# Stage Y on the two halves of TensorE: pairs of 48-row matmuls of 47 columns in place of single 112-row matmuls of 94

## The chip, the core and the metric

The kernel runs on one core of a Trainium2 chip. The metric is the device time of one execution in microseconds (us); lower is better. Executions of one kernel agree within about 0.4% of their median (one set of eleven runs of the kernel before: 794.43 to 799.02 around 796.20); a run far above the others, at a lower granted clock, is called slow and is left out.

## The reference

Eight batches of 3008 tokens with 256 features go through a filter in frequency space along the tokens, then each token through a two-layer network with a squared ReLU.

```python
X = np.fft.rfft(x, axis=1)                     # x: (8, 3008, 256)
Y = X * (filt_r + 1j * filt_i)[None]
y = np.fft.irfft(Y, n=3008, axis=1)
h = np.maximum(y.reshape(-1, 256) @ w_in, 0.0)   # w_in: (256, 2048)
out = (h * h) @ w_out                            # w_out: (2048, 256)
```

## The kernel before

The Fourier transforms are matrix products: 3008 = 64 x 47, and the inverse ends in stage Y, a transform of length 47 for each of the 64 values of n1. Its input, per n1, is 48 rows (24 frequencies, real and imaginary) of 256 features. Everything is in float16 with float32 sums.

Stage Y takes two n1 at a time, an even and an odd one. Their rows lie one above the other in a tile of 112 partitions (48, then 16 of zeros, then 48), and a table of 112 x 94 with zeros in half of its places keeps the two apart: 47 columns belong to the even n1 and 47 to the odd one, interleaved.

```python
def read_z(b, c, ks=(0, 1)):
    zt = ztiles[c]                                    # [112, 8, 256]
    v = dZ[b].rearrange("(q j) d -> q j d", j=NM)
    for k in ks:
        nc.sync.dma_start(out=zt[64 * k:64 * k + 48],
                          in_=v[48 * k:48 * k + 48, 8 * c:8 * c + 8, :])

def unit_y(b, n):                                     # n = 0..15 in each batch
    g, dt = divmod(n, 2)
    ...
    ps = psF(f"psY_{b}_{n}")                          # one PSUM bank (in the prologue, every other from psO)
    ...
    for jj in range(4):
        nc.tensor.matmul(ps[:, 94 * jj:94 * jj + 94],
                         zt[:, 4 * (g % 2) + jj, dt * 128:(dt + 1) * 128],
                         sSY, start=True, stop=True)
    ...
    if dt == 0 or (b == 0 and g > 5):
        nc.scalar.copy(out=o, in_=pv)                 # 376 columns
    else:
        nc.vector.tensor_copy(out=o, in_=pv)
```

A batch has 16 units of four matmuls. There are two psF banks, and stages A, B and P use the same two. The units are wedged between the pieces of the two network layers. One token group of 512 tokens has eight slots; a slot is four matmuls of the first layer, then what is planned for its place 0, then eight matmuls of the second layer (of the group before), then what is planned for its place 1:

```python
for s in range((NG + 1) * SLOTS):
    ffn_g1(g, k)          # 4 matmuls of 512 columns, into psH; then a relu on ScalarE
    run(work, s, 0)
    ffn_g2(g - 1, k)      # 8 matmuls of 256 columns, into psO
    run(work, s, 1)
    ffn_out(g - 1, k)
    ffn_sq(g, k)          # the square, on VectorE
```

So nearly every unit of stage Y has full-array matmuls on both sides.

## Time and profile before

| kernel before | |
|---|---|
| time, median of 3 runs | 795.54 us (795.02 to 796.49) |
| TensorE busy | 98% of the span |
| VectorE, ScalarE busy | 69%, 70% |
| stage Y: matmuls, weight loads | 512, 512 |
| one unit of four on the chain | 0.17 us |
| copies out of PSUM | 128 of 376 columns |

The busy times of engines other than TensorE cost nothing here, and the busy time of stage Y's matmuls (42.3 us) counts time that they share with their neighbours. What to read is the chain, which gives to each piece only the time by which it pushed the end. The lines are in the prediction.

### The profile page before, as it was taken

To read this page: it belongs to the slowest core of one execution; us is meant where nothing else is said; L and a number is where in the kernel's file an instruction comes from. 1 tells how busy PE (TensorE), PEld (TensorE's weight loads), DVE (VectorE), ACT (ScalarE), POOL (GpSimd) and SP (SyncE) were. 2 spreads that over 40 slices of the span, in tenths; PEclk is the share of its full clock that TensorE was granted. 3 is DMA by queue.
4 is the path that set the end of the run, shared out by engine and by line. 5 is a ranking of instruction groups with operands and counts; after the bars stand their busy time and mean duration, and the time that the engine had idled before them with its cause. 6 is when DMAs were issued, how large, how long until landed. Compare 5 with 4: busy or idle time off the path is not lost.

```text
span 795.8 us, 14801 instructions
## 1 busy us (share of the span) xinstructions
PE 783.1 (98%) x6102; PEld 553.7 (70%) x6102; DVE 552.2 (69%) x898; ACT 554.9 (70%) x708; POOL 24.4 (3%) x27
## 2 busy tenths in 40 slices
PE   8989999999999999999999999999999999999998
PEld 5846677667676676867778676776777667776666
DVE  6946995579855897559965699557985589554342
ACT  3856776767777677767777677676776767766664
POOL 3710000000000000000000000000000000000000
PEclk9989999999999999999999999999999999999999
DMA  9994555336724467055471555525563342511111
GB/s 352 361 277 134 130 151 139 92 126 165 202 58 107 158 165 181 30 164 151 124 183 49 171 153 137 129 71 156 156 170 97 87 142 80 123 48 41 40 41 54
DMA packets 88139, 107.32 MB, mean 135 GB/s; under 512 B 6288, under 2 KB 78864, under 8 KB 83856
## 3 DMA queue, kind: packets, MB, share of 16 engines
q1 hardware_dynamic: 87864, 106.19, 46.9%
q8 instruction: 48, 0.79, 0.4%
q10 hardware_dynamic: 144, 0.18, 0.1%
q14 instruction: 19, 0.16, 0.1%
q0 software_dynamic: 64, 0.00, 0.0%
HBM read 58.12 MB, written 48.23 MB: 134 GB/s over the span
## 4 chain that ended last, share of the span: by engine, by line
PE 93%; DMA 3%; ACT 1%; DVE 1%; issue 0%; POOL 0%; SPq 0%; ACTq 0%; DVEq 0%; POOLq 0%
PE psO L577 40%; PE psH L560 39%; PE psA L359 3%; PE psY L530 3%; PE psB L443 2%; PE psP L494 2%; PE warm L274 1%; DMA ut<-dU 1%; DMA xw<-in_x_dram 1%; PE psf L293 1%; DMA dZ<-ze 1%; ACT h L564 1%; PE psf L296 0%; DMA dU<-u 0%; PE psA L380 0%; ACT sF L303 0%
## 5 line engine op out<-in xcount | busy, mean ns | idle before, releaser
L564 ACT ACTIVATE h<-psH 128x1024 f16<-128x1024 f32 x376 | 385.2, 1025 | 189.7 <-PE psH L560 188.2
L577 PE MATMUL psO<-sWout,h 128*128 128x256 f16 x3008 | 388.6, 272 | 0.0
L560 PE MATMUL psH<-yt,sWin 128*128 128x512 f16 (+7 forms) x1728 | 386.9, 351 | 1.7 <-DVE yt L539 0.8
L577 PEld LDWEIGHTS <-h 128*128 128x128 f16 x3008 | 290.6, 98 | 77.3
L568 DVE TENSOR_TENSOR h<-h 128x1024 f16<-128x1024 f16 x376 | 253.7, 685 | 100.8 <-ACT h L564 99.2
L560 PEld LDWEIGHTS <-sWin 128*128 128x128 f16 x1728 | 159.5, 98 | 101.7 <-issue 3.5
L451 DVE TENSOR_TENSOR prod<-psB,sF 128x1024 f16<-128x1024 f32 x84 | 102.4, 1219 | 5.9 <-PE psB L443 5.6
L539 DVE CAST yt<-psY 128x376 f16<-128x376 f32 x62 | 33.9, 549 | 57.4 <-PE psY L530 57.4
L365 DVE CAST u<-psA 96x512 f16<-96x512 f32 x50 | 34.3, 687 | 47.3 <-PE psA L359 45.1
L496 ACT CAST ze<-psP 128x512 f16<-128x512 f32 x84 | 49.2, 586 | 17.8 <-PE psP L494 15.9
L588 ACT COPY ost<-psO 128x512 f32<-128x512 f32 (+1 forms) x96 | 55.7, 580 | 6.7 <-PE psO L577 5.3
L530 PEld LDWEIGHTS <-zt 112*128 112x128 f16 x512 | 34.9, 98 | 12.1 <-issue 2.0
L530 PE MATMUL psY<-sC,zt 112*128 112x94 f16 x512 | 42.3, 205 | 0.6 <-DMA zt<-dZ 0.3
L465 DVE TENSOR_TENSOR yf<-prod,yf 128x512 f16<-128x512 f16 x84 | 35.7, 425 | 2.9
L443 PE MATMUL psB<-ut,sSB 128*128 128x256 f16 x192 | 36.5, 272 | 0.6 <-DMA ut<-dU 0.5
L359 PE MATMUL psA<-x,sC 94*96 94x512 f16 x96 | 36.6, 382 | 0.0
L443 PEld LDWEIGHTS <-sSB 128*128 128x128 f16 x192 | 18.6, 98 | 20.9 <-issue 1.7
L494 PE MATMUL psP<-yf,sSP 128*128 128x256 f16 x168 | 32.1, 273 | 0.2 <-ACT yt L537 0.2
L537 ACT CAST yt<-psY 128x376 f16<-128x376 f32 x66 | 30.7, 468 | 1.1 <-PE psY L530 0.6
L338 DVE CAST x<-x 94x2048 f16<-94x2048 f32 x24 | 29.2, 1216 | 0.0
L363 ACT CAST u<-psA 96x512 f16<-96x512 f32 x50 | 28.6, 572 | 0.0
L458 DVE COPY yf<-prod 64x512 f16<-64x512 f16 x84 | 24.3, 289 | 2.9
(63 smaller groups left out, 255.9 us busy)
## 6 DMA issues: line engine op xcount, KB each, us to landing
x<-in_x_dram SPq DMA_DIRECT2D x20, 768.0 KB
zt<-dZ SPq DMA_DIRECT2D x64, 192.0 KB
dU<-u SPq DMA_DIRECT2D x28, 384.0 KB
dZ<-ze SPq DMA_DIRECT2D x28, 384.0 KB
out_dram<-ost SPq DMA_DIRECT2D x66, 128.0 KB
out_dram<-ost SPq DMA_DIRECT2D x31, 256.0 KB
ut<-dU SPq DMA_DIRECT2D x7, 1024.0 KB
xw<-in_x_dram SPq DMA_DIRECT2D x4, 1024.0 KB
```

The source lines that it names most:

```text
L359: nc.tensor.matmul(ps[0:96, :], sSA, x16s[(b, c)][:, m, :], start=True, stop=True)
L443: nc.tensor.matmul(ps[:, i * D:(i + 1) * D], sSB[:, 2 * p + i, :], uts[b][:, 2 * p + i, :], start=True, stop=True)
L451: nc.vector.tensor_mul(out=prod, in0=ps.rearrange("p (a d) -> p a d", d=D).unsqueeze(1).to_broadcast([128, 2, 2, D]), in1=sF[:, :, 2 * p:2 ...
L465: nc.vector.tensor_add(out=yf, in0=prod[:, 0], in1=yf)
L494: nc.tensor.matmul(ps[:, i * D:(i + 1) * D], sSP[:, 2 * p + i, :], yf[:, i, :], start=True, stop=True)
L496: nc.scalar.copy(out=zes[(b, c)][:, 2 * i6:2 * i6 + 2, :], in_=ps.rearrange("p (a d) -> p a d", d=D))
L530: nc.tensor.matmul(ps[:, 94 * jj:94 * jj + 94], zt[:, 4 * (g % 2) + jj, dt * 128:(dt + 1) * 128], sSY, start=True, stop=True)
L560: nc.tensor.matmul(ps[:, i, o:o + n], sWin[:, dt, jt * 128:(jt + 1) * 128], yts[b][:, dt, r:r + n], start=(dt == 0), stop=(dt == 1))
L564: nc.scalar.activation(out=h2[:, 2 * s:2 * s + 2, :], in_=ps, func=AF.Relu)
L568: nc.vector.tensor_mul(out=v, in0=v, in1=v)
L577: nc.tensor.matmul(pso[g][:, t % 2, :], h2s[g][:, jt, t * 128:(t + 1) * 128], sWout[:, jt, :], start=(jt == 0), stop=(jt == NJT - 1))
L588: nc.scalar.copy(out=ost[:, h0:h0 + step, :], in_=pso[g][:, h0:h0 + step, :])
```

## The change

The intent is to stop multiplying with zeros. The even n1 keeps partitions 0 to 63, the odd one 64 to 127, and each gets a matmul of 48 rows and 47 columns of its own. By the Trainium skill ("TensorEngine Tiling (Array Packing)", Overview and Gotcha 1) TensorE can work as two halves where 64 rows or fewer are summed, and the halves must write to different banks. So an even and an odd matmul may run at the same time: 47 columns of streaming in place of 94. A unit takes both psF banks, one for each half, and to fill them it takes eight n1 pairs rather than four. A batch has eight units in place of 16.

```diff
-    SY = np.zeros((32, 2, 2, N2, 2))
+    SP = SP.transpose(0, 1, 2, 4, 3, 5)              # order of rows of the stage before
+    SY = np.zeros((NC, 2, N2))
 ...
-    C0[:, 1376:1470] = SY.reshape(128, 94)
+    for i in range(2):
+        C0[64 * i:64 * i + 48, 1376:1376 + N2] = SY.reshape(48, N2)
 ...
-    for t in ztiles:
-        nc.vector.memset(t[32:64], 0.0)
 ...
-        for jj in range(4):
-            nc.tensor.matmul(ps[:, 94 * jj:94 * jj + 94],
-                             zt[:, 4 * (g % 2) + jj, dt * 128:(dt + 1) * 128],
-                             sSY, start=True, stop=True)
+        for j in range(8):
+            for i in range(2):
+                p = slice(64 * i, 64 * i + 48)
+                nc.tensor.matmul(ps[i][:, N2 * j:N2 * j + N2],
+                                 zts[(b, c)][p, j, dt * 128:(dt + 1) * 128],
+                                 sSY[p], start=True, stop=True)
 ...
+        engs = (nc.scalar.copy, nc.vector.tensor_copy)
+        for i in range(2):
+            (engs[0] if b == 0 and c == 3 else engs[i])(
+                out=o[:, 2 * c + i], in_=ps[i][:, 0:376].rearrange("p (j a) -> p a j", j=8))
 ...
-            for n in range(4, 16):
-                put(n if n < 8 else n + 2 if n < 12 else 2 * n - 7, n % 2, unit_y, 0, n)
+            for n in range(2, 8):
+                put((4, 6, 10, 12, 17, 20)[n - 2], 1, unit_y, 0, n)
 ...
-                put(44 + n // 2, n % 2, unit_y, b, n)
+                put(44 + n, 0, unit_y, b, n)
```

(Cut: the reads of Z with the new row order, the choice of banks in the prologue, and the plan of batch 1.)

More of the change, by code (lines that the diff above doesn't have):

```diff
@@ L84, in _build_consts @@
                 SP[1, f, c, i, 1] = sg * cs
-    SY = np.zeros((32, 2, 2, N2, 2))
+    SP = SP.transpose(0, 1, 2, 4, 3, 5)
+    SY = np.zeros((NC, 2, N2))
     for c in range(NC):
         th = 2 * np.pi * c * n2 / N2
-        for i in range(2):
-            SY[c + c // 12 * 4, i, 0, :, i] = np.cos(th)
-            SY[c + c // 12 * 4, i, 1, :, i] = -np.sin(th)
+        SY[c, 0] = np.cos(th)
+        SY[c, 1] = -np.sin(th)
     PF = np.zeros((128, 6, 2, 2, 32))
@@ L205 @@
     sSA = sC0[0:94, 1280:1376]
-    sSY = sC0[0:112, 1376:1470]
+    sSY = sC0[:, 1376:1376 + N2]
     ident = sC0[:, 576:704]
@@ L504, with read_z @@
     ztiles = [const.tile([112, 8, D], F16, name=f"zt_{c}") for c in range(4)]
-    for t in ztiles:
-        nc.vector.memset(t[32:64], 0.0)
-    def read_z(b, c, ks=(0, 1)):
+    def read_z(b, c):
         zt = ztiles[c]
-        v = dZ[b].rearrange("(q j) d -> q j d", j=NM)
-        for k in ks:
-            nc.sync.dma_start(out=zt[64 * k:64 * k + 48],
-                              in_=v[48 * k:48 * k + 48, 8 * c:8 * c + 8, :])
+        v = dZ[b].rearrange("(q i j) d -> i q j d", i=2, j=NM)
+        for i in range(2):
+            nc.sync.dma_start(out=zt[64 * i:64 * i + 48], in_=v[i, :, 8 * c:8 * c + 8, :])
@@ L514, in read_z @@
         zts[(b, c)] = zt
     def unit_y(b, n):
-        g, dt = divmod(n, 2)
+        c, dt = divmod(n, 2)
         if n == 0:
             yts[b] = p_y.tile([128, 2, S], F16, tag="yt", name=f"yt_{b}")
-        zt = zts[(b, g // 2)]
-        if not prologue[0]:
-            ps = psF(f"psY_{b}_{n}")
+        if prologue[0] and dt:
+            ps = [psO(f"psY_{b}_{n}_{i}").rearrange("p a d -> p (a d)") for i in range(2)]
         else:
-            ps = psF(f"psY_{b}_{n}") if dt == 0 else psO(f"psY_{b}_{n}").rearrange("p a d -> p (a d)")
+            ps = [psF(f"psY_{b}_{n}_{i}") for i in range(2)]
@@ L526, in unit_y @@
         if prologue[0]:
-            for k in range(2):
-                nc.tensor.matmul(ps[:, 128 * k:128 * k + 128], zero, zero, start=True, stop=True)
-        for jj in range(4):
-            nc.tensor.matmul(ps[:, 94 * jj:94 * jj + 94],
-                             zt[:, 4 * (g % 2) + jj, dt * 128:(dt + 1) * 128],
-                             sSY, start=True, stop=True)
-        r, t = g // 2 * 2, g % 2 * 4
-        o = yts[b].rearrange("p d (r a t) -> p d r a t", r=8, t=8)[:, dt, r:r + 2, :, t:t + 4]
@@ L535, in unit_y @@
-        pv = ps[:, 0:376].rearrange("p (j a i) -> p i a j", j=4, i=2)
-        if dt == 0 or (b == 0 and g > 5):
-            nc.scalar.copy(out=o, in_=pv)
-        else:
-            nc.vector.tensor_copy(out=o, in_=pv)
+            for k in range(4):
+                nc.tensor.matmul(ps[k % 2][:, 0:128], zero, zero, start=True, stop=True)
+        for j in range(8):
[4 more added lines that the diff above has]
+                                 sSY[p], start=True, stop=True)
@@ L542 @@
+        o = yts[b].rearrange("p d (r a t) -> p d r a t", r=8, t=8)[:, dt]
+        engs = (nc.scalar.copy, nc.vector.tensor_copy)
+        for i in range(2):
+            (engs[0] if b == 0 and c == 3 else engs[i])(
+                out=o[:, 2 * c + i], in_=ps[i][:, 0:376].rearrange("p (j a) -> p a j", j=8))
     h2s, pso = {}, {}
@@ L640, in fft_plan @@
                     put(r, 1, load_x, b + 1, c + 2)
-        for n in range(16):
+        for n in range(8):
             if b == 1:
-                put(38 + n // 2 if n > 3 else 39, n % 2, unit_y, b, n)
+                put((39, 39, 40, 41, 42, 43, 44, 45)[n], n % 2, unit_y, b, n)
             else:
-                put(44 + n // 2, n % 2, unit_y, b, n)
+                put(44 + n, 0, unit_y, b, n)
         return plan
@@ L718 @@
         write_u(1, c)
-    for n in range(4):
+    for n in range(2):
         unit_y(0, n)
```

## The prediction

> **What bounds the kernel now.** I read the page first: busy shares, then the chain that ended last, then the costliest groups.
>
> ```profile
> PE 783.1 (98%) x6102; PEld 553.7 (70%) x6102; DVE 552.2 (69%) x898; ACT 554.9 (70%) x708; POOL 24.4 (3%) x27
> ...
> PE 93%; DMA 3%; ACT 1%; DVE 1%; issue 0%; POOL 0%; SPq 0%; ACTq 0%; DVEq 0%; POOLq 0%
> ...
> L539 DVE CAST yt<-psY 128x376 f16<-128x376 f32 x62 | 33.9, 549 | 57.4 <-PE psY L530 57.4
> ...
> L530 PEld LDWEIGHTS <-zt 112*128 112x128 f16 x512 | 34.9, 98 | 12.1 <-issue 2.0
> L530 PE MATMUL psY<-sC,zt 112*128 112x94 f16 x512 | 42.3, 205 | 0.6 <-DMA zt<-dZ 0.3
> ...
> L537 ACT CAST yt<-psY 128x376 f16<-128x376 f32 x66 | 30.7, 468 | 1.1 <-PE psY L530 0.6
> ```
>
> TensorE is busy 98% of the span and is 93% of the chain; VectorE and ScalarE stand at 70%. So time of TensorE is time of the kernel, and stage Y (line 530) is 512 matmuls on 112 rows with 94 columns, each behind its own weight load. Its 42.3 us busy are not its cost: a single matmul is shown as 205 ns, but they overlap each other and their neighbours. What one costs on the path is read from the chain, in a stretch of the steady part:
>
> ```profile
> by line: PE psO L577 43.8%; PE psH L560 43.7%; PE psY L530 13.3%
> ...
> 223.29 0.17 PE psY L530 x4
> 223.46 0.88 PE psO L577 x8
> 224.34 0.17 PE psY L530 x4
> 224.51 0.88 PE psH L560 x8
> ...
> 232.86 0.87 PE psH L560 x8
> 233.74 0.87 PE psO L577 x8
> ```
>
> The columns are start, length, what. The chain is TensorE alone, without a hole. Four matmuls of stage Y take 0.17 us, some 42 ns each; eight of 256 columns take 0.88, so 110 ns each. The difference, 68 ns over 162 columns, is 0.42 ns a column; 94 columns are then 39 ns and 3 ns are left as a fixed part. So stage Y streams already: its weight loads, shown as 98 ns each, are wholly hidden. Its cost on the path is 512 x 42 = 21.4 us, 2.7% of 795.5. That is the whole prize if the stage cost nothing.
>
> How fast can a load and a matmul follow each other? Between 127 and 140 us a batch border falls inside a token group, and half of the eight matmuls of a piece have 64 columns only:
>
> ```profile
> L560 PE MATMUL psH<-yt,sWin 128*128 128x448 f16 x24 | 6.0, 352 | 0.0
> L560 PE MATMUL psH<-yt,sWin 128*128 128x64 f16 x24 | 2.8, 192 | 0.3 <-DVE yt L539 0.3
> ...
> 130.69 0.88 PE psH L560 x8
> ```
>
> Such a piece has 4 x 448 + 4 x 64 = 2048 columns, as many as eight of 256, and takes the same 0.88 us. So a pair of load and matmul goes through in about 64 x 0.42 + 3 = 30 ns with nothing added: a load of 128 columns repeats in 30 ns or less. How much less the trace can't say.
>
> **What the Trainium skill says.** "TensorE: Matmul & The Clock Gate", Back-to-back issue gap, gives N / 2.4 + 2.5 ns for a warm matmul; 94 columns make 41.7, and the trace has 42. It agrees. The same page, LDWEIGHTS, gives P / 1.2, thus 107 ns for 128 columns; the 98 ns of the records are near it, but loads repeat within 30 ns here, so as a rate it does not hold in this trace. The same page, Part 3 (Packing small matmuls), says that matmuls on different row groups run concurrently, with starts some 4 ns apart, and that a load overlaps a running matmul when the row groups differ. No run here shows that yet: nothing in this kernel has 64 rows or fewer. "TensorEngine Tiling (Array Packing)", Key Properties, says that changing the tiling mode drains TensorE, without a figure; its Gotcha 1 says that row tiles must write different banks, which is why the change takes two.
>
> **The change part by part.**
>
> TensorE, removed: 512 loads and 512 matmuls of 94 columns on 112 rows, half of whose products are with zeros: 21.4 us. Added: 1024 loads of 128 columns on 48 rows and 1024 matmuls of 47 columns, alternating between rows 0 to 63 and 64 to 127. One alone would take 47 x 0.42 + 3 = 23 ns. If both of a pair run at once and loads stay hidden, 512 pairs x 23 = 11.8 us: a gain of 9.6. That is the floor of the time, 786. I don't expect all of it: a pair now needs two loads and two matmuls issued in 23 ns, while the densest that the trace shows is one of each in 30. If loads of the two halves overlap so that a pair takes those 30 ns, it is 15.4 us and the gain is 6. This is my main case.
>
> Switching in and out of the half mode: 64 units, each between full-array matmuls, so some 128 changes. If a change lets the pipeline run dry, it exposes part of the 205 - 39 = 166 ns by which a matmul's record is longer than its streaming. Each 10 ns per change is 1.3 us. I put in 15 ns as a weighted mean of "nothing" and "a real drain": +2.
>
> Evictions: 128 units with one of 376 columns become 64 with two. Number, size and split (66 on ScalarE, 62 on VectorE: batch 0's last quarter still goes to ScalarE alone) stay; both old and new read PSUM with a stride, the new write is contiguous. 549 and 468 ns should stay; both engines are off the path. No gain.
>
> Banks: a unit now takes both psF buffers at once. From batch 2 on there is one unit a slot (2.09 us: 0.88 twice and 0.17 twice), always at the same place, and its ScalarE copy waits for a relu of 1.02 us and then takes 0.47: done some 1.6 us after the unit's start, before the next one. No wait. In batch 1's plan, though, two units of batch 0 (slots 17 and 20) meet stages B and P, which use the same two buffers. Before, even a one-buffer unit made stage P wait there:
>
> ```profile
> 82.75 1.22 DVE L451 TENSOR_TENSOR prod<-psB,sF 128x1024 f16<-128x1024 f32 x1
> 83.06 0.47 ACT L537 CAST yt<-psY 128x376 f16<-128x376 f32 x1
> ...
> 83.58 0.38 PE L494 MATMUL psP<-yf,sSP 128*128 128x256 f16 x2 [0.21 <-ACT yt L537]
> ```
>
> A two-buffer unit waits for the product of 1.22 us, and stage P then for a copy on ScalarE: an estimated 0.5 to 1 us twice. Against that, the first units of batch 1 now leave by both engines at once rather than two by VectorE one after the other. Net +1.
>
> The rest: the zeroing of four tiles (3.6 us of VectorE in the first 6 us, where it waits for input anyway) goes; the reads of Z keep 64 transfers of 192 KB with the same 4 KB pieces, since only the order of rows in the tables moved; the eight zero matmuls of the prologue remain eight. All 0.
>
> Sum: -6 + 2 + 1 = -3, from 795.5 to 792.5. The likeliest single outcome (no drain, waits small) is -5 to -6, near 790; I place the prediction between, at 791.
>
> **The rivals.**
>
> First, loads become the bound. If two loads of one pair go one after the other at 30 ns each, a pair takes 60 ns: 512 x 60 = 30.7 us, a loss of 9.3, with waits 806. If a load takes 20 ns, 512 x 40 = 20.5, and nothing is won. For it: twice the loads, and TensorE's loader then has to repeat faster than any record of before. Against it: 30 ns is an upper bound, and the skill has loads of different row groups in parallel.
>
> Second, the mode change drains. At 100 ns a change, 128 x 0.1 = 12.8 us eats the gain and more: about 803. For it: the skill's sentence, and units are wedged one by one between full-array pieces, so nothing amortises it beyond 16 matmuls. Against: no full stop is needed if only rows are regrouped, and different row counts (94, 112, 120, 128) follow each other without a hole now.
>
> Third, bank waits on TensorE in every batch rather than in two slots. If each of the 56 units outside the prologue and batch 0 lost 0.2 us, that would be 11 us, about 801. The 0.4 us of slack that I worked out speak against it.
>
> **Range and chances.** Main case without a drain, 786 to 791: 45%. Concurrency with a real drain, 792 to 803: 25%. No concurrency to speak of, 796 to 805: 20%. Both bad: 10%, up to 815. The middle is 791, and 785 to 804 should hold it 8 times in 10. Faster by over 2% means below 779.6, a gain of 16 out of a stage that costs 21: more than twice what perfect pairing gives, 1%. Slower by over 2% means above 811.4, which needs both rivals at once: 6%. Within 2%: 93%.
>
> **What would show it.** In the chain of the changed kernel a steady unit of sixteen matmuls should take about 0.24 us (0.18 if perfect, 0.33 if nothing is won, 0.48 with serial loads) against 0.33 for the two old units. Starts of the two matmuls of a pair should lie a few ns apart. The first matmul after each unit should follow without a hole; a hole of 50 ns or more at each border is the drain. In the list of waits, TensorE on the copies of yt should stay near 1 to 3 us in all; over 5 means that the banks are the cause. Evictions should keep 549 and 468 ns. I am wrong if steady units are cheap and the time still does not fall, or if the change outside stage Y is over 3 us.

## The result, and the profile after

The changed kernel takes 802.31 us (median of four runs, 801.85 to 802.88) against 796.01 us (median of four, 795.02 to 797.88). The ratio is 1.0077, 95% interval 1.0056 to 1.0097: slower by about 6 us. A ratio here is the mean time of one kernel's fast runs over the mean of the other's fast runs of the same rounds, so it is not quite the ratio of the medians. The time lies inside the range that was predicted, but on the wrong side of the kernel before.

From the page of the changed kernel (the groups give busy time and mean ns, then the idle time of the engine before them and what ended it):

```profile
PE 784.8 (98%) x6614; PEld 544.6 (68%) x6614; DVE 553.5 (69%) x894; ACT 556.2 (70%) x708; POOL 24.3 (3%) x27
...
L535 DVE CAST yt<-psY 128x376 f16<-128x376 f32 x62 | 34.1, 550 | 44.5 <-PE psY L529 43.9
...
L535 ACT CAST yt<-psY 128x376 f16<-128x376 f32 x66 | 30.7, 468 | 4.7 <-PE psY L529 2.9
...
L529 PEld LDWEIGHTS <-zt 48*128 48x128 f16 x1024 | 17.9, 93 | 22.1 <-issue 19.6
...
L529 PE MATMUL psY<-sC,zt 48*128 48x47 f16 x1024 | 25.4, 181 | 2.1 <-DMA zt<-dZ 1.1
```

The copies out of PSUM are what they were: 66 of 468 ns and 62 of 550 ns. The 1024 matmuls are busy for 25.4 us in place of 42.3. Not all of that is overlap of the halves: the old matmuls in units of eight, in a run below, are busy for 32.2, since the records of a longer unit run into each other. But ahead of the weight loads stands a number that was not there: the loader idles for 22.1 us, 19.6 of it as "issue", which means that the profile shows nothing that it waited for. The loads of before had 2.0 us of it.

The chain of the changed kernel in the same stretch of the steady part as in the prediction (start, length, what):

```profile
225.33 0.30 PE psY L529 x16
225.63 0.98 PE psO L574 x8
226.61 0.87 PE psH L557 x8
227.48 0.30 PE psY L529 x16
227.79 0.98 PE psO L574 x8
```

Two numbers are to be seen. (The first layer's piece is x8 where a batch border splits its four matmuls.) A unit of sixteen takes 0.30 us where two old units took 0.33 to 0.34; that would be a gain. And the eight matmuls of the second layer that follow take 0.98 us where they took 0.88, although nothing in them changed; the first layer's piece, which has no unit of stage Y before it now, takes 0.87 as ever. So each unit pushes 0.10 us into its neighbour. 0.30 + 0.10 is 0.40 against 0.33: a loss of 0.07 us a unit, which can be followed through the trace of every batch as a step of 0.07 us per slot that has a unit.

In the trace the sixteen matmuls start in twos, 3 or 4 ns apart, and after the first two the twos follow each other at 25 ns. Eight twos are 0.20 us; so of the 0.30 some 0.10 are spent before the second pair. The loss thus sits at both borders of the unit: 0.10 us going in, 0.10 coming out.

A second thing shows in the list of waits and in the chain of slots 17 and 20:

```profile
PE psP L495 <- ACT yt L535: 1.1, 2, 0.6
...
PE psY L529 <- DVE prod L452: 1.0, 2, 0.7
```

```profile
79.45 1.15 DVE prod L452
80.60 0.04 issue
80.64 0.40 PE psY L529 x15
81.03 0.47 ACT yt L535
81.50 0.04 issue
81.55 0.38 PE psP L495 x2
```

The columns of the first are the total, the count and the longest. Twice, TensorE waits for VectorE to empty one of the two banks of the unit, and then stage P waits for ScalarE to empty the unit's own: 1.0 + 1.1 = 2.1 us. The kernel before has 0.5 us of waits for copies of yt at stages Y and P.

A third thing is small. The reads of Z have a new order:

```diff
-        v = dZ[b].rearrange("(q j) d -> q j d", j=NM)
+        v = dZ[b].rearrange("(q i j) d -> i q j d", i=2, j=NM)
 ...
-                              in_=v[48 * k:48 * k + 48, 8 * c:8 * c + 8, :])
+            nc.sync.dma_start(out=zt[64 * i:64 * i + 48], in_=v[i, :, 8 * c:8 * c + 8, :])
```

The first read of a batch used to take rows 0 to 47, which the first two of four writes of Z fill; now it takes every second row and needs all four. In batches 1 to 7 of the kernel before the first read is issued 0.6 to 2.6 us ahead of the second, in the changed kernel 0.35 to 0.42 us. TensorE then waits for Z at first units: 1.1 us in all in the changed kernel (the line of L529 above) against 0.3. No run changes this order alone, but it goes with the order in every trace of a fast run: 0.8 to 1.6 us in the seven with the new one, none to 0.3 in the four with the old one.

**The sum.** Pairing: eight old matmuls of 42 ns against eight pairs of 25 ns, 64 units: 64 x 136 ns = -8.7. Borders: 64 x 0.20 = +12.8. Bank waits: 2.1 - 0.5 = +1.6. Waits for Z: 1.1 - 0.3 = +0.8. Together +6.5, and 0.0077 x 796 is 6.1 (by the interval, 4.5 to 7.7).

### The profile page after: what moved, and what is told of

It is laid out like the page before. It is cut to its first block, busy times and chain, and to the rows that moved or that the text cites. A ratio compares the mean times of both kernels' runs of the same rounds, so it can differ in the third digit from the quotient of the medians.

```text
span 800.1 us, 15810 instructions
## 1 busy us (share of the span) xinstructions
PE 784.8 (98%) x6614; PEld 544.6 (68%) x6614; DVE 553.5 (69%) x894; ACT 556.2 (70%) x708; POOL 24.3 (3%) x27
## 4 chain that ended last, share of the span: by engine, by line
PE 91%; DMA 6%; DVE 1%; ACT 1%; issue 0%; POOL 0%; SPq 0%; ACTq 0%; POOLq 0%
PE psO L574 39%; PE psH L557 38%; PE psA L360 3%; PE psB L444 2%; PE psY L529 2%; DMA ut<-dU 2%; PE psP L495 2%; DMA zt<-dZ 2%; PE warm L275 1%; DMA xw<-in_x_dram 1%; DMA wout<-in_moe_w_out_dram 1%; DVE prod L452 1%; PE psf L294 1%; PE psf L297 0%; ACT sF L304 0%; PE psT L421 0%
## 5 line engine op out<-in xcount | busy, mean ns | idle before, releaser
L557 PEld LDWEIGHTS <-sWin 128*128 128x128 f16 x1728 | 162.1, 98 | 102.4 <-issue 1.7
L529 PEld LDWEIGHTS <-zt 48*128 48x128 f16 x1024 | 17.9, 93 | 22.1 <-issue 19.6
L529 PE MATMUL psY<-sC,zt 48*128 48x47 f16 x1024 | 25.4, 181 | 2.1 <-DMA zt<-dZ 1.1
```

Source lines behind the costliest of these rows:

```text
L529: nc.tensor.matmul(ps[i][:, N2 * j:N2 * j + N2], zts[(b, c)][p, j, dt * 128:(dt + 1) * 128], sSY[p], start=True, stop=True)
L557: nc.tensor.matmul(ps[:, i, o:o + n], sWin[:, dt, jt * 128:(jt + 1) * 128], yts[b][:, dt, r:r + n], start=(dt == 0), stop=(dt == 1))
```

## The experiments

Three theories were to be told apart. A: each change between the full array and the half mode holds TensorE up, as if it had to be emptied, some 0.1 us each way, and this is more than the pairing wins. B: the loss is one of banks, of units that take both at once. C: it is one of instructions, 1024 loads and matmuls in place of 512. All kernels below gave the right result unless said otherwise.

| run | what | median us (runs) | ratio to before, 95% interval |
|---|---|---|---|
| changed kernel | | 802.31 (4) | 1.0077 (1.0056 to 1.0097) |
| e1_full_array | new units and banks, old matmuls | 798.78 (6) | 1.0029 (1.0013 to 1.0044) |
| e2_rows48 | before, 48 rows | 820.59 (4) | 1.0298 (1.0279 to 1.0317) |
| e3_rows80 | before, 80 rows | 795.56 (4) | 0.9990 (0.9970 to 1.0010) |
| e4_not_paired | changed, halves in turn | 808.86 (4) | 1.0145 (1.0124 to 1.0167) |
| e5_one_more_change | changed, one full matmul inside | 817.19 (3 fast) | 1.0267 (1.0239 to 1.0295) |
| e6_moved_slots | changed, two units moved | 799.65 (6) | 1.0040 (1.0019 to 1.0060) |
| e7_merged | two units in one | 793.55 (6) | 0.9964 (0.9944 to 0.9984) |
| e8_slots_10_13 | control of the merged one | 799.07 (6) | 1.0044 (1.0026 to 1.0061) |
| e9_before_slots | before, slots moved | 796.53 (6) | 1.0000 (0.9982 to 1.0018) |
| e10_merged_again | as e7 | 792.85 (6) | 0.9965 (0.9946 to 0.9984) |

Differences between two kernels of different rounds are taken from these ratios, times 796 us. Each ratio is good to about 0.2%, so such a difference is good to some 2 us either way.

### The new units with the old matmuls

```diff
-        for j in range(8):
-            for i in range(2):
-                p = slice(64 * i, 64 * i + 48)
-                nc.tensor.matmul(ps[i][:, N2 * j:N2 * j + N2], zts[(b, c)][p, j, ...], sSY[p], ...)
+        for k in range(2):
+            for j in range(4):
+                nc.tensor.matmul(ps[k][:, 94 * j:94 * j + 94], zts[(b, c)][:, 4 * k + j, ...], sSY, ...)
```

(With it go the table of 112 x 94, the zeroing of the tiles, and the order in which the copies read the bank.)

> The changed kernel with its units of twice the size, its two banks per unit and its plan, but with the old matmuls: 94 columns on 112 rows over the full array, four per bank. Theory A (each change between the full array and the half mode empties TensorE, some 0.10 us going in and 0.09 to 0.10 coming out, 0.2 us per unit, which is more than the 0.13 us per unit that pairing wins): the chain shows 0.33 us per unit and no longer piece after it, and the time falls to 796 to 798, with only the bank waits of two units of batch 0 left (about 2 us). Theory B (the loss comes from units that take both banks at once): the time stays at 801 to 803. Theory C (1024 loads are the loss): also 796 to 798, so this run does not part A from C.

Its chain:

```profile
225.37 0.34 PE psY L530 x8
225.70 0.87 PE psO L576 x8
226.58 0.87 PE psH L559 x8
```

0.34 us for a unit, and no longer piece after it. The time is 3.8 us under the changed kernel (1.0077 - 1.0029) and still 2.3 us over the kernel before; 798.78 lies just above the 796 to 798 that were expected. What is left is not bank waits alone: the list of waits has 0.9 us at the banks of the two units of batch 0, but also 1.6 us for the reads of Z, whose new order this run keeps. So B holds for at most about 2 us and not for the rest. A and C both survive this run.

### The mode alone, and its control

The kernel before, where stage Y reads 48 of its 112 rows, and then 80 (both give wrong results):

```diff
-                             zt[:, 4 * (g % 2) + jj, dt * 128:(dt + 1) * 128],
-                             sSY, start=True, stop=True)
+                             zt[0:48, 4 * (g % 2) + jj, dt * 128:(dt + 1) * 128],
+                             sSY[0:48], start=True, stop=True)
```

> The kernel before with one thing changed: stage Y reads 48 of its 112 rows (a wrong result on purpose). Same 512 loads and matmuls of 94 columns, same units, banks and plan, nothing paired. Theory A: 128 units go in and out of the half mode, about 126 of them alone between full-array matmuls, at 0.2 us each: plus 25 us, 820 to 823. Theories B and C: nothing that they name has changed, so 796.

> The control of the run with 48 rows: stage Y of the kernel before on 80 of its 112 rows (wrong result on purpose), which is over half of the array. All theories: 795 to 797. If the row count as such mattered, this would lie between 796 and the time of the run with 48 rows.

The chain with 48 rows, then with 80:

```profile
222.36 0.27 PE psY L530 x4
222.63 0.98 PE psO L577 x8
223.61 0.27 PE psY L530 x4
223.88 0.97 PE psH L560 x4
```

```profile
222.13 0.17 PE psY L530 x4
222.30 0.88 PE psO L577 x8
223.17 0.17 PE psY L530 x4
223.34 0.87 PE psH L560 x8
```

This is the cleanest pair. Instructions, banks and plan are those of the kernel before in both; only the number of rows differs, and no matmul has a partner. With 80 rows every piece is as it was. With 48 each unit takes 0.27 in place of 0.17, and each neighbour 0.98 or 0.97 in place of 0.88 or 0.87: 0.10 us in, 0.10 us out. 126 units x 0.20 would be 25 us; measured are 0.0298 x 796 = 23.7. The cost that theory A names is shown, and C is out, since no load was added. The step lies between 48 and 80 rows; the runs do not say where.

The traces of the two runs also say how TensorE is held up. With 80 rows a weight load starts 1 or 2 ns after the start of the matmul before it, at the units as elsewhere, and so runs under it. With 48 rows the first load of a unit starts 201 ns after a last matmul of 256 columns, which takes 110 ns, and the first load after a unit 133 ns after one of 94 columns, which takes 42: 91 ns in which nothing starts, both times. The load's own matmul is recorded as starting 4 or 5 ns after it. So the time is not one in which a load runs in the open; load and matmul are both held back. Whatever the width of the last matmul on the way in, from 128 to 512 columns, the load starts 72 ns before that matmul's recorded end (an end that the profile models). This fits an emptying of TensorE; what inside it is emptied the runs do not say.

### Do the halves work at once?

```diff
-        for j in range(8):
-            for i in range(2):
+        for i in range(2):
+            for j in range(8):
                 p = slice(64 * i, 64 * i + 48)
```

> The changed kernel with the sixteen matmuls of a unit in another order: first the eight of the upper half, then the eight of the lower, so that neighbours use the same rows. Number of mode changes, loads, banks: all as in the changed kernel. If the pair's step of 25 ns comes from two row groups working at once, a matmul now takes 22 to 30 ns by itself, a unit 0.36 to 0.48 us instead of 0.20, and the time rises by 10 to 18 us, to 812 to 820. If the step of 25 ns has nothing to do with the alternation, it stays at 802.

```profile
227.35 0.42 PE psY L529 x16
227.77 0.98 PE psO L574 x8
228.75 0.87 PE psH L557 x8
```

The border after the unit is the same 0.10; the unit takes 0.42 in place of 0.30, and 64 x 0.12 is 7.7 us. Measured are 5.4 us by the ratios and 6.5 by the medians. The alternation therefore does buy time, but my size of 10 to 18 us was too large. I had expected 16 matmuls to take 16 steps. In the trace a half takes one matmul every 25 ns, as it does in the paired order; but the lower half's first matmul is recorded as starting before the upper half's last three, in 52 of the 54 units where the records tell the two halves apart by their waits. So the second half starts before the first is through, and the sixteen need about 0.32 us beyond the entry, not 0.40.

### One more change inside a unit

```diff
         for j in range(8):
+            if j == 4 and not prologue[0]:
+                nc.tensor.matmul(ps[0][:, 384:400], zero, zero[:, 0:16], start=True, stop=True)
             for i in range(2):
```

> The changed kernel with one more full-array matmul of 16 columns (zeros, into unused columns of the unit's own bank) after the eighth of the sixteen matmuls of a unit, in 62 of 64 units. Theory A: each such unit goes out of the half mode and back once more, so the time rises by 62 times about 0.2 to 0.24 us: plus 12 to 15 us, 814 to 818. If only the instruction counts, it costs some 25 ns each: plus 1.6 us, 804.

One of the four runs was slow (922 us, granted clock 0.851), and it was the one that was profiled, so no line of it is used. The three fast runs are 816.76, 817.19 and 819.82: by the ratios 15.1 us over the changed kernel, 0.24 us for each of the 62 added matmuls. A matmul of 16 columns does not cost that in itself: with its load, one of 64 columns took 30 ns in the kernel before. It is one more way out and back.

### The two units that meet other stages

```diff
-                put((4, 6, 10, 12, 17, 20)[n - 2], 1, unit_y, 0, n)
+                put((4, 6, 10, 12, 21, 26)[n - 2], 1, unit_y, 0, n)
```

> The changed kernel with the two units of batch 0's last quarter moved from slots 17 and 20, where stages B and P use the same two banks, to slots 21 and 26, where neither is placed. TensorE's waits there on the product of stage B and on the copies of yt add to about 2.1 us in the trace of the changed kernel, so all theories expect a gain of 1.5 to 2.5 us: 800. No gain would mean that the time waited there comes back elsewhere in that stretch, where VectorE is nearly full.

A gain of 2.9 us by the ratios, with some 2 us of noise, and neither of the two waits that were shown from the changed kernel is in its list any more. Theory B is right for this part of the loss, and for this part alone.

### Fewer stays in the half mode

If the border costs 0.2 us however long the stay is, longer stays should pay. A unit is limited by its banks, so this one borrows a pair from the first layer:

```diff
+    def unit_yy(b, c):
+        h = psH(f"psYY_{b}_{c}")
+        ps = [[psF(f"psY_{b}_{c}_{i}") for i in range(2)], [h[:, 0, :], h[:, 1, :]]]
+        for dt in range(2):
+            for j in range(8):
+                for i in range(2):
+                    p = slice(64 * i, 64 * i + 48)
+                    nc.tensor.matmul(ps[dt][i][:, N2 * j:N2 * j + N2],
+                                     zts[(b, c)][p, j, dt * 128:(dt + 1) * 128],
+                                     sSY[p], start=True, stop=True)
+        ...                                   # four copies, ScalarE and VectorE in turn
 ...
+            for c in range(2, 4):
+                put((10, 13)[c - 2], 2 - c + 1, unit_yy, 0, c)
 ...
+        for c in range(4):
+            put((39, 41, 43, 45)[c] if b == 1 else 44 + 2 * c, 0, unit_yy, b, c)
```

> The changed kernel with two units in one for 30 of the 32 quarters but batch 0's first two: 32 matmuls in one go over four banks (the two that stage Y had and one pair of the FFN's), every second slot, and batch 0's last two quarters in slots 10 and 13. Theory A: 30 fewer stays in the half mode at 0.2 us, minus 6 us, and about 2 us more from the bank waits of batch 0 that fall away: 793 to 796, which would be level with or slightly under the kernel before. If the FFN has to wait for the pair of banks that it lent, up to 2 us of this is lost. Without theory A: 800 to 802.

The ratio is 0.9964: 9.0 us under the changed kernel, and 2.9 us under the kernel before. Its plan for batch 0 is new too, so it was run again beside two controls on one chip: the changed kernel with that plan but without the merging, and the kernel before with its last quarter in slots 12 and 13. (Both also share the copies of batch 0's last quarter between the two engines.)

```diff
-                put((4, 6, 10, 12, 17, 20)[n - 2], 1, unit_y, 0, n)
+                put((4, 6, 10, 11, 12, 13)[n - 2], 1, unit_y, 0, n)
```

> The changed kernel, unmerged, with batch 0's last two quarters where the merged kernel has them (slots 10 to 13, evictions by both engines). It is the control for the merged kernel: the only difference left is that 30 quarters take two stays in the half mode instead of one. If the merging is what gained (30 times 0.2 us), this run is at 799 to 801, 6 us over the merged kernel of the same call. If the new slots gained, it is at 794 to 796 too.

```diff
-                put(n if n < 8 else n + 2 if n < 12 else 2 * n - 7, n % 2, unit_y, 0, n)
+                put(n if n < 8 else 10 + (n - 8) // 2, n % 2, unit_y, 0, n)
```

> The kernel before with the last quarter of batch 0 in slots 12 and 13 instead of 17 to 23 and evictions by both engines. TensorE waited 0.2 us for those units in the trace of before, so 795 to 796.5: level with before. If it came to 793 or 794, the lead of the merged kernel over the kernel before would be one of the plan and not of the half mode.

> The merged kernel once more, on the same chip as its two controls. Worked out from the chain of its first trace: a quarter takes 0.61 us with its drain against 0.67 in the kernel before, 30 times 0.06 is 2 us: 0.2 to 0.4% under the kernel before, 793 to 794.5.

The chain of the merged kernel:

```profile
224.28 0.87 PE psH L578 x8
225.16 0.30 PE psY L549 x16
225.46 0.20 PE psYY L549 x16
225.66 0.98 PE psO L595 x8
226.64 0.87 PE psH L578 x8
```

The first sixteen take 0.30 as before, but the second sixteen, which go into the borrowed banks without leaving the half mode, take 0.20: eight pairs at 25 ns and nothing else. This is the pairing as it was meant, seen without its borders. A quarter costs 0.30 + 0.20 + 0.10 = 0.60 us, against four old units of 0.17. The merged kernel repeats at 0.9965, as expected. Its first control is at 1.0044, so merging is worth 0.0079 x 796 = 6.3 us, for 30 borders in and 30 out less: 0.21 us for a pair of borders, as in every other run. The second control is at 1.0000, so the lead over the kernel before is not one of the plan.

## Why the prediction was wrong

**What bounds the kernel: right.** TensorE stayed busy for 98% of the span, and every term of the sum above is work of TensorE or a wait of TensorE.

**Stage Y's cost on the path, 21.4 us: right**, and with it the ceiling.

**Pairing, predicted 30 ns a pair and -6 us: mechanism right, size a little small.** Measured 25 ns a pair, -8.7 us. The first rival, loads one after the other at 20 to 30 ns each, is out: two loads and two matmuls pass in 25 ns.

**Mode changes, predicted 15 ns each and +2 us: this is the step that failed.** Measured 0.10 us each way, +12.8 us. The chain's unit of sixteen is therefore 0.30 us and not the predicted 0.24, and the sign that I had named, a hole of 50 ns or more at each border, is there as 91 ns in which no load and no matmul starts. I had named the drain as the second rival, with 100 ns and 12.8 us, which is what came; but in the sum I put a weighted mean of nothing and a real drain. A cost of this kind is either there or not, and the mean of the two is a value that neither case would show. What spoke against it in the prediction was that row counts of 94, 112, 120 and 128 follow each other without a hole. The run with 80 rows shows why that was no evidence: all of these lie on the same side of the step. The kernel before held no case of the other side, so its trace could not decide the matter, and a sentence of the Trainium skill ("TensorEngine Tiling (Array Packing)", Key Properties) was all there was. The cost that it points to came, and it deserved the main place rather than a quarter.

**Bank waits, predicted +1 net, two units of 0.5 to 1 us each: right place, right mechanism.** 2.1 us in the trace, 2.9 by the run that moved the two units. The third rival, bank waits in every batch, did not come: the list of waits has none.

**Copies, reads and zeroing, predicted 0:** the copies kept 468 and 550 ns. For the reads, 0 was too low: size and number of the transfers stayed, but the first of each batch now has to wait for more writes, some 0.8 us in all. The reads and the zeroing were not tried by themselves.

**The range** of 785 to 804 held because it had been drawn from the rivals as well; the point of 791 and the sign did not. That the second rival's 803 is so near to 802.31 is partly luck: its pairing was 2.7 us too small, and its waits, with those for Z, 1.4 us too small the other way.

## What to carry to other kernels

Before splitting TensorE into halves, count the borders and not the matmuls: here a stay in the half mode cost 0.20 us however long it was, a pair of 47-column matmuls won 17 ns, and so, by this estimate, a stay had to hold at least twelve pairs (200 / 17 = 11.8) to pay. Eight lost, sixteen won. A matmul that merely has few rows pays the border without winning anything, so pad it over the step (80 rows were enough here) unless it has a partner, and where a cost is either there or not, predict one of the two cases and not their mean.

## What the Trainium skill lacked or had wrong

- "TensorEngine Tiling (Array Packing)", Key Properties, says that changing the tiling mode drains TensorE and gives no figure. Here it is 0.10 us going in and 0.10 us coming out: 0.17 to 0.27 for the unit and 0.88 to 0.98 for its neighbour with 48 rows, and 0.21 us for a pair of borders when merging takes 30 of them away.
- The same page offers the tiling for small contractions and does not say that a lone matmul of few rows pays for it too. With 48 rows and no partner the kernel lost 23.7 us; with 80 rows nothing.
- The same page has no rule for how many matmuls a stay must hold. Here eight pairs lost 0.07 us a unit and sixteen pairs won 0.07 us a quarter.
- "TensorE: Matmul & The Clock Gate", Part 3, says that matmuls start and end in program order. In the run with the halves in turn, the records have the lower half's first matmul starting before the upper half's last three. Starts of a pair some 4 ns apart, as the page says, were seen: 3 or 4 ns.
- The same page, Part 1, says that the time from start to start never drops below about 25 ns, and does not say there that this holds for each half by itself. Here each half kept to it, 25 ns a step, but the starts of the two halves lay 3 or 4 ns apart. (The formula of its Back-to-back issue gap gives an estimate of 22 ns for 47 columns, and the page's own floor stands above it. The prediction's best case of 23 ns a pair, worked out from the trace, overlooked that floor.)
